# Windowed attention with global tokens, then a softplus MLP: indices spread by a product, q and k in one tile, V of batch 1 rounded by its transfer, and a new recorded order

## The chip, the cores and the metric

The kernel runs on one core of one Trainium2 chip. The core has five engines with an instruction stream each: PE (TensorE, matrix products), DVE (VectorE), ACT (ScalarE), POOL (GpSimd) and SP (SyncE, here used to issue transfers). The metric is the device time of one execution in microseconds; a comparison uses medians. Times inside an execution are read from a hardware profile of one execution, counted from the start of its span.

## The reference

Attention over 8 batches × 8 heads × 576 tokens × 64 dims: a token sees the 32 tokens to each side of it and 8 global tokens (the indices are an input), and the global tokens see all. Its output, 4608 tokens of 512 values, goes through a two-layer MLP with softplus.

```python
scores = scale * np.matmul(q, k.transpose(0, 1, 3, 2))
mask = np.abs(pos[:, None] - pos[None, :]) <= window       # window = 32
mask = mask | is_global[:, None] | is_global[None, :]
attn = np.exp(scores - max) / (sum + 1e-09)                # where the mask holds
x = (attn @ v).transpose(0, 2, 1, 3).reshape(B * S, H * D) # 4608 x 512
h = x @ w_in                                               # 512 x 2048
g = np.maximum(h, 0.0) + np.log1p(np.exp(-np.abs(h)))      # softplus
out = g @ w_out                                            # 2048 x 512
```

## The kernel before

**Tiles.** The tokens are cut into 36 "pairs" n of four blocks of 32 tokens (all 8 heads of a pair together) and nine MLP tiles m of 512 tokens, four pairs each. A batch has 18 blocks, so that batch 1 begins in the second tile.

**One pair.** PE makes the scores s (L1061, with a mask product at L1045 or L1055 for the first pairs). DVE adds the mask (L1065), takes the maximum m (L1076 or L1078), and after ACT's exponential (L1097 or L1101) the sum sm (L1108) and its reciprocal rs (L1110). POOL subtracts the maximum (L1084) and multiplies with the reciprocal (pn, L1116). DVE transposes the weights (pt, L1125), and PE multiplies them with V (xo, L1227): vb holds V of the window, vg the result of the global tokens.

**The global tokens.** Their q and k rows are picked by products with 0/1 matrices. Batches 0 and 1 are transposed on PE (tr, L843 and L846) and picked there with `hot` (L849, L853). From batch 2 on, DVE transposes q and k; PE picks the rows with `pick` (`pck`, L872: 18 products for k and 18 for q), a copy takes them to `picked`, and 32 small products with `place` (`put`, L886) lay them out; they are copied to `qg` (`gev`) and into the keys (`fill`). The global scores are sg (L959), their product with V is ov (L985).

**One MLP tile.** The four xo are copied to xT (L719). PE makes h in 16 chunks of 4 products (L1262), ACT the softplus g (L1268), PE the second product o in 4 × 16 products (L1273), and the copies osb go out by transfers (L1285). `PIECED` names the tiles whose h are made in pieces, as their pairs come in: tile 0 in pieces of 1, 2 and 1 pairs, tile 1 of 1 and 3, the others whole.

**Transfers.** SP issues the loads of q, k and v. Batches 0 and 1 come in parts (`load_part`, L511 for 256 tokens, L515 for the last 64), later batches in 32-token blocks (`load_qk`, L456; `load_v`, L466). POOL issues transfers through its software queue: V of batch 0, which is rounded to bf16 on the way (`load_rounded`, L461), the first weights win (L1325, four pieces) and the second weights wout (L1329, four pieces). V of batch 1 and later is loaded as it is into `stage` and cast on an engine (L719). Two tiny transfers called `trail` (L750, `follow`) read a piece of the weights, so that SP waits there: the first for the third piece of win ahead of the parts of batch 1, the second for the second piece of wout ahead of V of batch 1. A copy called `seen` (L1406, the job "landed") makes POOL wait for a part of batch 1 ahead of wout: the last 64 tokens of q, third among batch 1's loads in SP's order.

**The order.** All work is recorded as jobs, with engines that may run it, costs and due times, in class `_Order`. A table `ORDER` (one number for each job and the engine chosen) then fixes the order of everything. Where PE has nothing to do in the first microseconds, `fill_in` puts products without use (warm, L727), whose operand is the tile `pgt`.

## Time and profile before

| what | us |
|---|---|
| median of 3 runs (lowest, highest) | 333.86 (333.33, 334.97) |
| the profiled execution, its own time | 334.75 |
| its span in the profile | 333.0 |
| PE busy / DVE busy / ACT busy / POOL busy | 318.6 / 223.4 / 228.4 / 193.6 |
| first h of the MLP | 29.49 |
| scores of batch 1's first whole pair | 46.22 |
| PE idle before ov of batch 1 | 1.46 |
| moved by DMA, whole span | 42.14 MB |

The span runs from the first to the last instruction; 1.75 us of the profiled execution lie outside it. Rows of a timeline read: start, duration, engine, line, operation, output<-input, count, and in brackets how long the engine was idle before and what ended that. Durations of PE rows overlap, since its products are pipelined: what a product costs is read from start to start. Rows of a table of windows read: the stretch, its length, then busy time and count on PE, on PE's weight loads, on DVE, ACT and POOL, the granted clock, the DMA share and GB/s. The granted clock was 0.984 of full speed over the span, and full from 24 us on in every window that is shown.

### The profile page before, as it was taken

The numbers are of one execution on the slowest core, as the hardware profiler recorded it, in microseconds if no ns is written. First come the engines' busy times: TensorE is split into PE (matmuls) and PEld (weight loads), VectorE is DVE, ScalarE is ACT, GpSimd is POOL, SyncE is SP. The second block draws the span as 40 slices with busy tenths as digits, with TensorE's granted clock in tenths as the row PEclk, the third lists the DMA queues.
The fourth block names the chain that finished last, engine by engine and source line by source line (L and its number), as shares of the span: only waits on it lengthen the run. The fifth ranks groups of instructions, "written<-read, shape, count | busy, mean of one in ns | idle before, by whom it ended". The sixth has DMA issues, their size and how long they took to land.

```text
span 333.0 us, 12043 instructions
## 1 busy us (share of the span) xinstructions
PE 318.6 (96%) x5273; PEld 170.8 (51%) x5273; DVE 223.4 (67%) x393; ACT 228.4 (69%) x448; POOL 193.6 (58%) x171
## 2 busy tenths in 40 slices
PE   6978899899999999999999999999999999999995
PEld 2736785465555455544454445445544454454453
DVE  7689679895897899992884299497966757530000
ACT  3889866796787879388746664997369666743622
POOL 5976308694677778879639459587447445600000
PEclk9589999999999999999999999999999999999999
DMA  6999899999889999999950799520210002000102
GB/s 179 165 160 214 198 183 175 152 143 230 141 135 175 214 184 142 225 204 156 213 114 33 125 181 219 114 65 33 98 64 33 33 2 96 2 33 31 65 24 103
DMA packets 168796, 42.14 MB, mean 127 GB/s; under 512 B 153256, under 2 KB 165800, under 8 KB 168744
## 3 DMA queue, kind: packets, MB, share of 16 engines
q1 hardware_dynamic: 154888, 26.63, 44.7%
q0 software_dynamic: 10944, 11.08, 16.4%
q10 hardware_dynamic: 2912, 3.67, 3.1%
q8 instruction: 41, 0.67, 0.8%
q14 instruction: 11, 0.09, 0.1%
HBM read 36.71 MB, written 9.44 MB: 139 GB/s over the span
## 4 chain that ended last, share of the span: by engine, by line
PE 75%; DMA 6%; DVE 5%; SPq 4%; POOL 4%; issue 2%; ACT 2%; POOLq 0%
PE h L1262 32%; PE o L1273 32%; PE xo L1227 3%; DMA stage<-in_q_dram 3%; PE s L1061 3%; SPq L456 3%; DMA win<-in_moe_w_in_dram 2%; PE tr L843 1%; SPq L466 1%; POOL pn L1116 1%; PE ov L985 1%; DVE sm L1108 1%; DVE st L1065 1%; DMA gi<-in_global_idx_dram 1%; DVE m L1078 1%
## 5 line engine op out<-in xcount | busy, mean ns | idle before, releaser
L1273 PE MATMUL o<-wout,g 128*128 128x512 bf16 (+1 forms) x592 | 140.5, 374 | 0.3 <-ACT g L1268 0.3
L1262 PE MATMUL h<-xT,win 128*128 128x512 bf16 (+3 forms) x768 | 139.6, 326 | 0.9 <-ACT xT L719 0.8
L1268 ACT ACTIVATE g<-h 128x512 bf16<-128x512 f32 (+3 forms) x192 | 83.2, 504 | 44.1 <-PE h L1262 41.6
L1262 PEld LDWEIGHTS <-win 128*128 128x128 bf16 x768 | 66.6, 98 | 60.6 <-issue 2.2
L1273 PEld LDWEIGHTS <-g 128*128 128x128 bf16 x592 | 55.5, 98 | 60.7 <-ACT g L1268 2.0
L1116 POOL TENSOR_TENSOR pn<-st,rs 128x1024 bf16<-128x1024 f32 (+1 forms) x37 | 66.2, 1799 | 31.5 <-DVE rs L1110 23.5
L1084 POOL TENSOR_TENSOR st<-st,m 128x1024 f32<-128x1024 f32 x32 | 60.3, 1895 | 31.6 <-DVE m L1078 31.5
L1065 DVE TENSOR_TENSOR st<-s,mask 128x512 f32<-128x512 f32 x64 | 41.1, 674 | 12.2 <-PE s L1061 12.1
L1108 DVE TENSOR_REDUCE sm<-st 128x8 f32<-128x1024 f32 x32 | 38.3, 1198 | 6.6 <-ACT st L1101 6.5
L1078 DVE TENSOR_REDUCE m<-st 128x8 f32<-128x1024 f32 x32 | 38.3, 1204 | 0.2
L1101 ACT ACTIVATE st<-st 128x1024 f32<-128x1024 f32 x32 | 33.3, 1059 | 1.6 <-POOL st L1084 1.5
L1125 DVE STREAM_TRANSPOSE pt<-pn 128x512 int32<-128x512 int32 x36 | 24.5, 691 | 9.1 <-POOL pn L1116 9.0
L719 ACT COPY osb<-o 128x512 f32<-128x512 f32 (+1 forms) x27 | 15.7, 580 | 17.8 <-PE o L1273 15.9
L719 ACT CAST xT<-xo 128x512 bf16<-128x512 f32 (+3 forms) x25 | 11.0, 512 | 19.1 <-PE xo L1227 19.1
L719 POOL CAST vb<-stage 128x1152 bf16<-128x1152 f32 x12 | 13.6, 1144 | 14.3 <-DMA stage<-in_v_dram 10.2
L1268 ACT ACT_TABLE_LOAD x14 | 18.0, 1283 | 0.2
L1285 POOL DMA_DIRECT2D out_dram<-osb x24 | 13.7, 572 | 4.6 <-DMA stage<-in_k_dram 3.5
L719 DVE CAST xT<-xo 128x512 bf16<-128x512 f32 (+3 forms) x23 | 11.3, 533 | 7.2 <-PE xo L1227 7.2
L1061 PEld LDWEIGHTS <-qx 64*32 64x32 bf16 x1152 | 10.3, 92 | 9.0 <-issue 6.0
L1061 PE MATMUL s<-kx,qx 64*32 64x128 bf16 x1152 | 14.7, 225 | 0.0
L716 POOL TENSOR_SCALAR qb<-stage 128x1152 bf16<-128x1152 f32 (+1 forms) x8 | 11.0, 1385 | 5.8 <-DMA stage<-in_q_dram 2.6
L1101 ACT ACT_TABLE_LOAD x11 | 14.1, 1283 | 0.2
(125 smaller groups left out, 296.8 us busy)
## 6 DMA issues: line engine op xcount, KB each, us to landing
stage<-in_v_dram SPq DMA_DIRECT2D x56, 144.0 KB, 3.8
stage<-in_k_dram SPq DMA_DIRECT2D x48, 144.0 KB, 4.2
stage<-in_q_dram SPq DMA_DIRECT2D x48, 144.0 KB, 3.6
out_dram<-osb POOLq DMA_DIRECT2D x24, 256.0 KB, 3.4
out_dram<-osb ACTq DMA_DIRECT2D x11, 256.0 KB, 2.0
stage<-in_q_dram SPq DMA_DIRECT2D x4, 512.0 KB, 5.5
win<-in_moe_w_in_dram POOLq DMA_DIRECT2D x8, 256.0 KB, 6.1
wout<-in_moe_w_out_dram POOLq DMA_DIRECT2D x4, 512.0 KB, 9.0
```

Source lines behind the costliest of these rows:

```text
L719: {"ACT": nc.scalar.copy, "DVE": V.tensor_copy, "POOL": nc.gpsimd.tensor_copy}[e](out, in_)
L1061: nc.tensor.matmul(out=PS["s", n, g][quad(a), x, :], lhsT=qx[b % 2][rows(g), a, j * BL:(j + 1) * BL], rhs=kx[b % 2][rows(g), a, e0 * BL:(e ...
L1065: V.tensor_tensor(out=PS["st", n][:, h, :, :], in0=PS["s", n, h][:, :, :], in1=mask[:, h, j0:j0 + PB, :, :].rearrange("p j s i -> p j (s i ...
L1078: V.reduce_max(out=m[:], in_=flat(PS["st", n], h0, h1), axis=AX)
L1084: on(e).tensor_tensor(out=t, in0=t, in1=over(PS["m", n, y][:], SL * BL), op=OP.subtract)
L1101: nc.scalar.activation(out=t, in_=t, func=AF.Exp)
L1108: V.reduce_sum(out=sm[:], in_=flat(PS["st", n], h0, h1), axis=AX)
L1116: on(e).tensor_tensor(out=PS["pn", n][:, :, :, h0:h1].rearrange("p x s h -> p h x s"), in0=PS["st", n][:, h0:h1], in1=PS["rs", n, y][:].re ...
L1125: V.transpose(out=bass.AP(base.tensor, base.offset, ap=[list(base.ap[0]), [2 * STEP, PB // 2], [STEP + BL // 2, 2], [1, SL * BL]]), in_=PS ...
L1262: nc.tensor.matmul(out=h[:, :], lhsT=w_in_t[c // 4][:, kd, c % 4 * P:(c % 4 + 1) * P], rhs=PS["xT", m][:, kd, lo:hi], start=(kd == 0), sto ...
L1268: nc.scalar.activation(out=PS["g", m, c][:, lo:hi], in_=PS[key][:, lo_of(c, hi - lo)], func=AF.Softplus)
L1273: nc.tensor.matmul(out=PS["o", m, ns, a][:, :], lhsT=PS["g", m, kf][:, ns * P:(ns + 1) * P], rhs=w_out_t[kf // 4][:, kf % 4, a:z], start=( ...
```

## The change

1. The global indices come by one DMA of one partition on ACT's queue (it was one of 128 partitions on SP's). DVE splits them into bytes (`make_bytes`), PE spreads them to all partitions by a product with ones (`make_spread`), and `make_hot` puts the bytes together again. The first part of q is now first on SP; k's first part was on ACT's queue.
2. q and k lie in one tile `qk`. From batch 2 on, 16 products pick rows of both (256 columns) and four do the last chunks (128 columns): 20 instead of 36. `put` is one product of 256 columns with a 128×128 `place` in the stead of 32. A copy (`back`) takes the result to `placed`, a DVE transpose (`gev`) to `qkg`, and `fill` reads that.
3. V of batch 1 is rounded by its transfer: eight DMAs of POOL behind the fourth wout, and no cast. K of batch 2 waits on SP, by the second trail, for the fourth wout.
4. The gate of wout (`landed`) reads the part 1 of k, second among batch 1's loads in the new order.
5. `PIECED` has tile 2 as pieces of 1 and 3 pairs.
6. Warm products read a tile of their own (`idle`).
7. Some subtractions and products pn of tiles 0 to 3 may lie on DVE. Constants of the recorder are changed, and the table `ORDER` is new.

```diff
-    PIECED = {0: (1, 2, 1), 1: (1, 3)}
+    PIECED = {0: (1, 2, 1), 1: (1, 3), 2: (1, 3)}
     ORDER = (
-        4, 88, 52, 131, 9, 57, 112, 14, 137, 92, 116, 107, 62, 142, 148, 102, 188, 190, 126, 121, 217, 201, 97, 19,
+        52, 62, 57, 4, 65, 141, 126, 9, 136, 107, 147, 131, 72, 98, 102, 196, 152, 227, 112, 158, 200, 206, 122, 14,
...
-    gi = const([P, 2 * NG], I32, "gi")
-    qb = const([P, HG * NC, BL, 2], BF16, "qb")
-    kb = const([P, HG * NC, BL, 2], BF16, "kb")
+    gi = const([1, 2 * NG], I32, "gi")
+    gb = const([1, 2 * NG], BF16, "gb")
+    ones = const([1, P], BF16, "ones")
+    qk = const([P, 2, HG * NC, BL, 2], BF16, "qk")
+    qb, kb = qk[:, 0], qk[:, 1]
...
+    idle = const([P, 512], BF16, "idle")
...
-    place = const([P, R, 2 * NG], BF16, "place")
+    place = const([P, P], BF16, "place")
...
-    load_part(0, 1, 0, nc.scalar)
-    nc.sync.dma_start(out=gi[:, :], in_=global_idx.rearrange("(one n) -> one n", one=1).bitcast(I32)
-                      .to_broadcast([P, 2 * NG]))
+    load_part(0, 0, 0)
+    nc.scalar.dma_start(out=gi[:, :], in_=global_idx.rearrange("(one n) -> one n", one=1).bitcast(I32))
...
+    def make_bytes():
+        V.tensor_copy(gb[:].rearrange("p (n x) -> p n x", x=2),
+                      gi[:].bitcast(mybir.dt.uint8).rearrange("p (n x) -> p n x", x=8)[:, :, 0:2])
+
+    def make_spread():
+        PS["gi"] = psum(("gi",), [P, 512], FP32)
+        nc.tensor.matmul(out=PS["gi"][:, 0:2 * NG], lhsT=ones[:, :], rhs=gb[:, :], start=True, stop=True)
...
+    def add_rounded(b, deps):
+        T["cast", b, 2] = []
+        for c in range(R):
+            T["cast", b, 2].append(o.add({"POOL": (1360, 0)}, lambda e, c=c: load_rounded(b, c), T["cast", b, 2][-1:] or deps,
+                                         rank=-1, moves=1400, hold=0 if b or c else 8700))
+        T["load", b, 2] = T["cast", b, 2][-1]
...
+            def emit(e):
+                if b == EARLY and "led" not in T:
+                    T["led"] = True
+                    follow(1, w_out_t[KF // 4 - 1])
+                load_qk(nc.sync, b, w, (0, 2, 1, 3))
...
+        def pck(e):
+            PS[key] = psum(key, [P, 512], FP32)
+            x = qk[:].rearrange("p w (a c) i d -> p w a c i d", a=HG)
+            for t in range(2 * NC):
+                c, z = divmod(t, 2)
+                whole = t < 2 * NC - 2
+                for w in range(1 if whole else 2):
+                    n = t % R if whole else t % R + 2 * w
+                    w0, w1 = (0, 2) if whole else (w, w + 1)
+                    nc.tensor.matmul(out=PS[key][quad(n), w0 * P:w1 * P], lhsT=pick[:, c, z, :],
+                                     rhs=x[:, w0:w1, :, c, :, z] if whole else x[:, w, :, c, :, z], start=(t < R), stop=not whole)
...
+        def put(e):
+            nc.tensor.matmul(out=PS[key][:, 2 * P:4 * P], lhsT=place[:, :], rhs=picked[:].rearrange("p w d -> p (w d)"), start=True, stop=True)
+
+        def back(e):
+            copy(e, placed[:], PS[key][:, 2 * P:4 * P])
...
+                V.transpose(out=qkg[i][:].rearrange("p w a g -> p (w a g)"), in_=placed[:])
...
-            T["landed"] = o.add(pool(100), lambda e: nc.gpsimd.tensor_copy(seen[:, 0, :], natural(0, FULL)[:, 0:1]), [T["part", 1, 0, FULL]], rank=0)
+            T["landed"] = o.add(pool(100), lambda e: nc.gpsimd.tensor_copy(seen[:, 0, :], flat(stage[1])[:, 4 * HD - 1:4 * HD]), [T["part", 1, 1, 1]], rank=0)
```

The new table moves instructions at three places that matter below. The first is ACT's order around the first copy to xT, at 29 us: st, sm<-s, m are exponentials of tile 0, g the first softplus. Before:

```order
L971 ACTIVATE pg<-sg,gnb 128x256
L1097 ACTIVATE st,sm<-s,m 128x128 x24
L719 CAST xT<-xo 128x128 x3
L1268 ACT_TABLE_LOAD
L1268 ACTIVATE g_834<-h 128x128
```

and now:

```order
L995 ACTIVATE pg<-sg,gnb 128x256
L1121 ACTIVATE st,sm<-s,m 128x128 x16
L1020 ACTIVATE vg_75<-ov,grs 128x128
L739 CAST xT<-xo 128x128 x2
L1121 ACTIVATE st,sm<-s,m 128x128 x4
L1292 ACT_TABLE_LOAD
L1292 ACTIVATE g_914<-h 128x128
```

All 32 exponentials stood ahead of the xT casts; now 28 do, and the last four stand behind them, with vg ahead of them.

The second is SP's order from the first trail on (stage_60 is q, stage_61 k, stage_62 v). Before:

```order
L750 DMA trail<-win_127 1x2x1
L511 DMA stage_60<-in_q_dram 128x8x128
L511 DMA stage_61<-in_k_dram 128x8x128
L515 DMA stage_60<-in_q_dram 64x4x64 x2
L511 DMA stage_61<-in_k_dram 128x8x128
L515 DMA stage_61<-in_k_dram 64x4x64 x2
L511 DMA stage_60<-in_q_dram 128x8x128
L750 DMA trail<-wout_130 1x2x1
L466 DMA stage_62<-in_v_dram 32x18x64 x8
L456 DMA stage_61<-in_k_dram 32x36x32 x8
```

and now:

```order
L769 DMA trail<-win_132 1x2x1
L518 DMA stage_61<-in_k_dram 128x8x128 x2
L518 DMA stage_60<-in_q_dram 128x8x128 x2
L522 DMA stage_60<-in_q_dram 64x4x64 x2
L522 DMA stage_61<-in_k_dram 64x4x64 x2
L769 DMA trail<-wout_137 1x2x1
L458 DMA stage_61<-in_k_dram 32x36x32 x8
```

The big parts now come first and the tails last, V of batch 1 is gone, and the second trail reads the fourth piece of wout. On POOL the eight V transfers stand behind the four wout, ahead of the first subtraction of batch 1 (L1084, then L1108). Before:

```order
L1406 COPY seen<-stage_60 128x1
L1329 DMA wout_129<-in_moe_w_out_dram 128x4x512
L1329 DMA wout_130<-in_moe_w_out_dram 128x4x512
L1329 DMA wout_131<-in_moe_w_out_dram 128x4x512
L1084 TENSOR_TENSOR st<-st,m 128x1024 x2
L1329 DMA wout_132<-in_moe_w_out_dram 128x4x512
L719 CAST vb_67<-stage_62 128x18x64
L1084 TENSOR_TENSOR st<-st,m 128x1024
L719 CAST vb_67<-stage_62 128x18x64
```

and now:

```order
L739 CAST qk<-stage_61 128x2x4x64
L1431 COPY seen<-stage_61 128x1
L1353 DMA wout_134<-in_moe_w_out_dram 128x4x512
L1353 DMA wout_135<-in_moe_w_out_dram 128x4x512
L1353 DMA wout_136<-in_moe_w_out_dram 128x4x512
L1353 DMA wout_137<-in_moe_w_out_dram 128x4x512
L463 DMA vb_68<-in_v_dram 32x18x64 x8
L1108 TENSOR_TENSOR st<-st,m 128x1024 x3
```

The fourth wout no longer stands behind two subtractions, both casts of V are gone, and a cast of k stands ahead of `seen`.

The third is PE at the placing product of batch 2 (each product stands with its weight load). Before, the first two of the 32 behind the products h:

```order
L1262 MATMUL h<-xT,win_127 128x384
L886 LDWEIGHTS picked
L886 MATMUL pick<-place,picked 32x8
L886 LDWEIGHTS picked
L886 MATMUL pick<-place,picked 32x8
```

and now, all of it:

```order
L1286 MATMUL h<-xT,win_131 128x384
L906 LDWEIGHTS place
L906 MATMUL pick<-picked,place 128x256
L1286 LDWEIGHTS win_131
L1286 MATMUL h<-xT,win_131 128x384
```

Where 32 products of 8 or 16 columns stood, there is one of 256, between products h of the same kind as before.

More of the change, by code (lines that the diff above doesn't have):

```diff
@@ L721 @@
     o = _Order(SLOTS, KINDS, 8)
-    idle = pgt[:].rearrange("p m i -> p (m i)")
     def fill_in(key, n):
@@ L1416 @@
     o.follow(ORDER)
-    for job in o.run(dict(PE=1200 if WARM else 3000, ACT=2600, DVE=2100, POOL=3400, DMA=2700)):
+    for job in o.run(dict(PE=1200 if WARM else 3000, ACT=2600, DVE=2100, POOL=3400, DMA=2000)):
         job["emit"](job["on"])
```

123 lines of the change are left out of this document (54 added, 69 removed), and 144 rows, old and new, of the table ORDER.

## The prediction

> **What bounds the kernel now.** I read the page first (busy time, then the chain that ended last).
>
> ```profile
> PE 318.6 (96%) x5273; PEld 170.8 (51%) x5273; DVE 223.4 (67%) x393; ACT 228.4 (69%) x448; POOL 193.6 (58%) x171
> PE 75%; DMA 6%; DVE 5%; SPq 4%; POOL 4%; issue 2%; ACT 2%; POOLq 0%
> ```
>
> PE is busy for 96% of the span and holds 75% of the chain. So time can be won in two ways only: fewer PE microseconds, or fewer stretches in which PE has nothing useful. Where those lie is seen by stage (PE busy is the second column) and in the list of what PE waited for.
>
> ```profile
> 28.00:40.00 12.00, 10.20 (x234) 8.78 (x226) 9.64 (x26) 10.20 (x40) 5.64 (x11) 1.00 0.95 231
> 40.00:46.00 6.00, 5.43 (x150) 5.12 (x151) 3.33 (x9) 4.50 (x13) 0.00 (x0) 1.00 1.05 159
> 54.00:62.00 8.00, 6.89 (x92) 3.92 (x91) 7.90 (x13) 7.70 (x15) 4.21 (x4) 1.00 0.97 157
> 104.00:320.00 216.00, 216.00 (x3393) 106.52 (x3377) 140.36 (x213) 147.51 (x230) 126.70 (x90) 1.00 0.51 107
> PE ov L985 <- DVE m L1078: 1.5, 1, 1.5
> PE o L1273 <- ACT g L1268: 0.3, 1, 0.3
> ```
>
> From 104 us on PE is never idle: only its own work counts there. The open time lies ahead: 1.8 us from 28 to 40, 0.57 from 40 to 46, 1.1 from 54 to 62, and the two later waits listed (1.5, 0.3), to which a third, of 0.54, comes at 76 us (row at tile 2, below). What bounds the early part is when the first h and the scores of batch 1 can start.
>
> ```profile
> 29.49 4.03 PE L1262 MATMUL h<-xT,win 128*128 128x128 bf16 x64 [0.79 <-ACT xT L719]
> 46.22 0.78 PE L1061 MATMUL s<-kx,qx 64*32 64x128 bf16 x64
> ```
>
> The first h starts at 29.49; the scores of batch 1 at 46.22. Between them PE has too little it may do, so **work that is put ahead of 46.22 is won, and a shift of 46.22 is lost or won whole**. The sum below is made at that point.
>
> **The change, part by part.**
>
> *The first 29 us.* The indices come in one packet and are spread by a product instead of a DMA to all partitions.
>
> ```profile
> 0.81 3.60 DMA gi<-in_global_idx_dram
> 9.04 0.61 PE L843 MATMUL tr<-ident,qb 128*128 128x128 bf16 x4 [2.77 <-POOL qb L716]
> ```
>
> The index transfer lasts until 4.41, and it stands first in the chain; the first transposes wait for q until 9.04. Now q's first part is ahead of everything on SP and the indices are on ACT's queue; against that stand a cast on DVE and a small product with its wait. Bounds: −1 (some of the 2.77) and +1 (the new steps, if the indices end last at the mask). I count it as nothing, since the first h hangs on ACT's exponentials, which come next.
>
> *The scores of batch 1.* They need its loads, the casts and the transposes.
>
> ```profile
> 28.77 0.42 ACT L1097 ACTIVATE st<-s,m 128x128 f32<-128x128 f32 x1
> 29.11 0.66 ACT L719 CAST xT<-xo 128x128 bf16<-128x128 f32 x3
> 21.23 0.45 DVE L975 STREAM_TRANSPOSE pgt<-pg 128x256 bf16<-128x256 bf16 x1 [1.36 <-PE warm L727]
> ```
>
> ACT casts xT at 29.11, right behind its last exponential (28.77, one every 0.34 us, 28.77 to 29.11). The new order puts the last four behind the xT casts: up to 4 × 0.34 = 1.4 us earlier. The warm matmuls get a tile of their own, so DVE no longer waits 1.36 us at 21.23. These two overlap, and batch 0's own loads and an added PE-to-DVE index step stand ahead of both; I take h at 28 to 28.5. SP's loads of batch 1 hang on the third piece of the first weights, whose place hardly changes; so of the gain I carry only **−0.7** to the scores. Bounds: −1.2 (all of the ACT gain but 0.2) and, where the loads are slowed, +4 and beyond (rivals).
>
> *Work put ahead of those scores.* Counted in PE's order, 84 products h of 128 columns, 44 of 256 and no o stood ahead of them; now 80, 56 and five o of 512. The price is
>
> ```profile
> 106.59 3.45 PE h L1262 x16
> ```
>
> 0.216 us for 512 columns, so 0.054 and 0.108 for the narrow ones: 12 × 0.108 + 5 × 0.216 − 4 × 0.054 = 2.2 us. There is room: PE's idle 1.8 + 0.57 without the 0.79 ahead of h is 1.6 us, an h that starts 1 to 1.5 us earlier makes it 2.6 to 3.1, and 2.2 with the 0.7 of the scores take 2.9. **−2.2**; bounds 0 (h not earlier, so the work itself pushes the scores) and −2.2.
>
> *V of batch 1 by POOL's transfers, and the gate of the second weights.*
>
> ```profile
> 54.27 12.21 SPq L456 DMA_DIRECT2D stage<-in_k_dram x8
> wout<-in_moe_w_out_dram POOLq DMA_DIRECT2D x4, 512.0 KB, 9.0
> vb<-in_v_dram POOLq DMA_DIRECT2D x7, 72.0 KB, 3.4
> 61.16 1.14 POOL L719 CAST vb<-stage 128x1152 bf16<-128x1152 f32 x1 [3.67 <-DMA stage<-in_v_dram]
> 62.35 0.80 PE L985 MATMUL ov<-vb,pgt 32*32 32x129 bf16 x72 [1.46 <-DVE m L1078]
> 10.27 5.69 POOL L461 DMA_DIRECT2D vb<-in_v_dram x8
> ```
>
> The 1.46 us are put down to DVE, but POOL's second cast of V ends at 61.16 + 1.14 = 62.30 and the product starts at 62.35: V was late. Now V comes rounded behind wout on POOL's own queue: eight issues of 5.69 / 8 = 0.71 us, hidden under POOL's idle time ahead of its first subtraction,
>
> ```profile
> 49.83 3.75 POOL L1084 TENSOR_TENSOR st<-st,m 128x1024 f32<-128x1024 f32 x2 [9.92 <-DVE m L1078]
> q0 software_dynamic: 1576, 1.57, 102.9%
> q0 software_dynamic: 4848, 0.71, 150.8%
> ```
>
> (uncovered they would cost up to 5.7 us of POOL). The four wout are 2.1 MB; from 40 to 50 us the software queue moved 1.57 MB (upper row), so 13.4 us; with batch 0's V it moved 0.71 MB from 12 to 19 (lower row), so the eight pieces, 0.59 MB, take 5.8. With wout from about 39.5 V is there near 59, ahead of 62. The wait of ov goes, and two casts (2.3 us) leave POOL, and K of batch 2 (54.27), now behind the last wout instead of V, starts about where it did, since wout ends near 53. The 0.5 and 0.3 us stalls go with the new order. Of 1.5 + 0.5 + 0.3 I book **−2.0**; bounds 0 and −2.3.
>
> The Trainium skill ("DMA: Bandwidth & Descriptors", section "Queues, rings and completion order") says that each DMA engine serves the queues with work in turn, packet by packet, so the loads on SP would go on beside wout at a packet's share. The trace so far speaks rather for starving, in the two rows from 56 to 59 us quoted under the rivals; what the rule makes of the time is the second rival.
>
> *Picks of batches 2 to 7.*
>
> ```profile
> 104.85 0.47 PE L872 MATMUL pick<-kb,pick 128*32 128x128 bf16 x18
> 105.55 1.04 PE L1273 MATMUL o<-wout,g 128*128 128x512 bf16 x4
> 109.97 0.37 PE L886 MATMUL pick<-place,picked 128*32 128x8 bf16 x32
> 110.27 0.39 PE L1273 MATMUL o<-wout,g 128*128 128x512 bf16 x1
> ```
>
> Picking takes 0.70 us for 36 (19 ns each: four run side by side), placing 0.30 for 32. The new 16 × 256 + 4 × 128 columns cost 0.49 us if they stream at the full rate (a quarter of 0.108 and 0.054 each) and 0.69 if width counts as the 19 ns do; the one placing matmul of 256 columns 0.11. Gain per batch 0.20 to 0.40, six batches 1.2 to 2.4: **−1.5**, since the 19 ns look like a price per instruction for the larger part. The new copy and DVE's transpose (an estimate: half of the transpose of pt whose row stands under the rivals) add some 1 us a batch to DVE and ACT, beside a PE that is full, with DVE at 67%; uncovered, a batch's global scores would come 1 us later.
>
> *Tile 2 in two pieces.*
>
> ```profile
> 65.13 0.23 PE L1227 MATMUL xo<-pt,vg 32*64 32x64 bf16 x8
> 65.75 1.47 PE L1273 MATMUL o<-wout,g 128*128 128x512 bf16 x6
> 76.08 0.38 PE L1227 MATMUL xo<-pt,vg 32*64 32x384 bf16 x8 [0.54 <-DVE pt L1125]
> 77.31 1.68 PE L1273 MATMUL o<-wout,g 128*128 128x512 bf16 x7
> 103.36 1.56 PE xo L1227 x143
> ```
>
> Tile 1 already goes so: its xo took 0.62 + 1.23 = 1.85 us against 1.56 whole: +0.3. Its 64 products h of 512 columns become 128 of 384 and 128; at 2 to 4 ns more for each pair, +0.2. **+0.5** (0.3 to 0.8).
>
> *Stalls of the re-made order.* Every engine's order is new (a few subtractions and products of tiles 0 to 3 may now lie on DVE too), and waits of this size cannot be read from an order: **+1.5**, as much as the largest stall of now; bounds 0 and 3.
>
> **Sum:** −0.7 − 2.2 − 2.0 − 1.5 + 0.5 + 1.5 = −4.4. The profiled execution took 334.75, with a span of 333.0; by the sum it becomes 330.35 and 328.6. The median shown, 333.86, lies 0.89 lower: **329.5**.
>
> **The rivals.**
>
> *Starved loads (slower).* The gate of wout moves from the third of batch 1's six loads to the second.
>
> ```profile
> 37.13 0.26 POOL L1406 COPY seen<-stage 128x1 f32<-128x1 f32 x1 [6.08 <-DMA stage<-in_q_dram]
> q1 hardware_dynamic: 1393, 0.60, 76.0%
> q0 software_dynamic: 419, 0.42, 90.8%
> q1 hardware_dynamic: 238, 0.05, 12.0%
> ```
>
> Now wout is let go at 37.13, issued at 37.59, and until 40.4 SP's queue still moved 0.60 MB (first queue row), so that the loads ended just as wout began. An earlier gate lets wout in near 39, with 0.15 to 0.5 MB of them open. From 56 to 59 us, with both queues loaded, SP got 0.05 MB beside 0.42 (last two rows), 17 GB/s: 0.25 MB take 15 us, until 54, and the scores come near 56, 10 us late: −4.4 + 0.7 − 1.5 (PE waits, so the others catch up) + 10 = +4.8, so **338.7**. It decides for slower as soon as the scores are more than 6.9 us late. Against it: only a rest may be open by then. Chance 0.13.
>
> *Turn by turn (the rule named above).* SP's packets from 37.6 to 40.4 were 0.60 MB / 1393 = 430 bytes, wout's 0.42 MB / 419 = 1000. With a turn each SP keeps three tenths of some 165 GB/s, 50: 0.25 MB take 5 us instead of the 1.2 at the 0.60 MB in 2.8 us of that row, 4 us more, of which 3 reach the scores: −4.4 + 0.7 − 1.5 + 3 = −2.2, **331.7**. Chance 0.14.
>
> *The gain is given back at tile 1 (no change).* From its scores to its xo, DVE was the bound (7.90 of 8 us busy from 54 to 62). If that chain stays as long, work put ahead leaves PE short at 76 us: without the −2.2, and with the waits of 0.54 and 0.3 still there, −4.4 + 2.2 + 0.8 = −1.4, **332.5**. Against it: two POOL casts are gone. Chance 0.12.
>
> *Late weights pt (slower).* Later tiles get their transposed weights with little to spare:
>
> ```profile
> 137.09 0.71 DVE L1125 STREAM_TRANSPOSE pt<-pn 128x512 int32<-128x512 int32 x1 [0.33 <-POOL pn L1116]
> 138.26 0.29 PE L1227 MATMUL xo<-pt,vg 32*64 32x192 bf16 x8
> ```
>
> 0.46 us here. PE work that shrinks comes earlier, POOL and DVE work doesn't; 1 us on each of seven tiles makes 329.5 + 7 = **336.5**. Against it: POOL is busy for 58% only. Chance 0.09.
>
> **How the numbers follow.** Forecast 0.52 (its own range 326.5 to 332.0), rivals 0.13, 0.14, 0.12, 0.09. A measurement of this kernel tells about 0.5%, 1.67 us: faster is below 332.2, slower above 335.5. Faster: the forecast and most of turn by turn, 0.52 + 0.13 = 0.65. Same: the third rival, 0.12, and the mild ends of the others, 0.03. Slower: starving and late weights, 0.13 + 0.09, less their mild ends, 0.20. The range leaves out the worst of starving and gains beyond the bounds: 326.0 to 336.5.
>
> **What would show it.** Right: first h before 28.6, the scores of batch 1 at 45 to 46, no wait of its ov, picks of batches 2 to 7 at 0.5 to 0.7 us, PE full from 80 us. Wrong: wout packets while SP's loads of batch 1 stand still, transposes of batch 1 waiting for casts of late parts; or xo of tiles 2 to 8 waiting for pt; or a wait of DVE or POOL in tile 1 that gives the lead back by 78 us.

## The result, and the profile after

| | kernel before | changed kernel |
|---|---|---|
| median (lowest to highest), us | 334.06 (333.33 to 334.97), 4 runs | 330.71 (329.47 to 331.85), 4 runs |
| profiled execution, its span, us | 334.75, 333.0 | 331.00, 329.3 |
| first h | 29.49 | 24.89 |
| scores of batch 1 | 46.22 | 45.41 |
| ov of batch 1 | 62.35, after 1.46 idle | 59.81, no wait |

The ratio is 0.9898, with a 95% interval from 0.9853 to 0.9942: faster by 1.0%. Medians, ranges and ratios here leave out executions that took over 1.5% longer than the fastest of the same kernel. The forecast was 329.5, its range 326.0 to 336.5.

The page of the changed kernel, busy time and the chain that ended last:

```profile
PE 311.0 (94%) x5007; PEld 171.1 (52%) x5052; DVE 228.1 (69%) x402; ACT 228.1 (69%) x468; POOL 198.6 (60%) x180
PE 74%; ACT 9%; DMA 8%; issue 2%; DVE 2%; POOL 2%; SPq 1%; ACTq 0%
```

Two readings need care. PE shows 5007 products but 5052 weight loads, and each product has its load: 45 records of products are missing, so PE's 311.0 us is too low, and small holes in its row are not all idle time. And DMA's part of the chain has grown from 6% to 8%, ACT's from 2% to 9%.

PE's waits in the changed kernel (total, times, longest), the largest ones and the one of h:

```profile
PE o L1297 <- issue: 2.9, 18, 0.2
PE xo L1251 <- ACT vg L1020: 2.3, 2, 1.9
PE xo L1251 <- issue: 1.7, 3, 0.7
PE tr L867 <- DVE qk L739: 1.5, 2, 0.8
PE o L1297 <- DMA wout<-in_moe_w_out_dram: 0.7, 1, 0.7
PE h L1286 <- DVE xT L739: 0.3, 1, 0.3
```

The 18 equal holes of 0.16 on o are missing records. The waits of ov for V and of o for g are gone from the list. "xo <- issue" is new: three holes of up to 0.7 us, 1.7 in all, in which PE waits for nothing that the profile shows.

The four stages, as windows (columns as before):

```profile
28.00:40.00 12.00, 11.36 (x278) 10.20 (x277) 7.86 (x25) 9.44 (x36) 6.60 (x10) 0.96 0.99 233
40.00:46.00 6.00, 4.84 (x139) 3.65 (x137) 2.90 (x9) 3.34 (x10) 1.01 (x3) 1.00 1.23 200
54.00:62.00 8.00, 7.79 (x145) 4.26 (x145) 7.18 (x11) 7.92 (x17) 7.54 (x5) 1.00 0.93 162
104.00:320.00 216.00, 211.66 (x3128) 106.48 (x3155) 142.46 (x217) 144.10 (x232) 126.13 (x88) 1.00 0.48 101
```

From 28 to 40 PE is busy 1.2 us more than before, from 54 to 62 0.9 more. (The clock of 0.96 in the first row: it was at half until 29.1 us, so that some of the 1.2 is slower products. More on the clock stands behind the experiments with V.) But from 40 to 46, just ahead of the scores of batch 1, it is busy 0.6 less: a new hole. Its cause is in the timelines of the changed kernel, PE's first h and scores, and DVE's cast of the last part of batch 1's k (a "tail" of 64 tokens) between them:

```profile
24.89 2.35 PE L1286 MATMUL h<-xT,win 128*128 128x128 bf16 x24
43.74 0.29 DVE L739 CAST qk<-stage 128x256 bf16<-128x256 f32 x1 [2.60 <-DMA stage<-in_k_dram]
45.41 0.78 PE L1085 MATMUL s<-kx,qx 64*32 64x128 bf16 x64
```

The first h is 4.6 us earlier than before, the scores only 0.81: DVE stood 2.60 us for the last tail. The DMA queues show why. Packets, MB and share of the changed kernel from 38 to 42 us:

```profile
q0 software_dynamic: 610, 0.61, 94.5%
q1 hardware_dynamic: 520, 0.13, 24.2%
```

and of the kernel before from 34 to 38 us, where SP's queue loads batch 1 with no wout beside it:

```profile
q1 hardware_dynamic: 1981, 0.79, 76.3%
```

Alone the loads move 1981 packets in 4 us; beside wout they move 520, about one for each of wout's 610. That is the round by packets that the Trainium skill describes ("DMA: Bandwidth & Descriptors", section "Queues, rings and completion order"), the second rival of the prediction; this trace agrees. The loads are not starved, as the first rival had it, but the tails' packets are small (0.13 MB / 520 = 250 bytes against 1000), so turn for turn they get a sixth of the bytes.

### The profile page after: what moved, and what is told of

It is laid out like the page before. It is cut to its first block, busy times and chain, and to the rows that moved or that the text cites. A ratio compares the mean times of both kernels' runs of the same rounds, so it can differ in the third digit from the quotient of the medians.

```text
span 329.3 us, 11571 instructions
## 1 busy us (share of the span) xinstructions
PE 311.0 (94%) x5007; PEld 171.1 (52%) x5052; DVE 228.1 (69%) x402; ACT 228.1 (69%) x468; POOL 198.6 (60%) x180
## 4 chain that ended last, share of the span: by engine, by line
PE 74%; ACT 9%; DMA 8%; issue 2%; DVE 2%; POOL 2%; SPq 1%; ACTq 0%
PE h L1286 33%; PE o L1297 32%; DMA wout<-in_moe_w_out_dram 4%; ACT st L1121 3%; PE xo L1251 3%; PE s L1085 3%; DMA stage<-in_k_dram 2%; DMA stage<-in_q_dram 2%; PE ov L1009 1%; ACT st L1125 1%; ACT g L1292 1%; PE pick L899 1%; ACT L1292 1%; ACT L1125 1%; POOL wout L1353 1%
## 5 line engine op out<-in xcount | busy, mean ns | idle before, releaser
L1286 PE MATMUL h<-xT,win 128*128 128x512 bf16 (+3 forms) x826 | 141.4, 316 | 1.2 <-DVE xT L739 0.3
L1297 PE MATMUL o<-wout,g 128*128 128x512 bf16 (+1 forms) x556 | 134.2, 373 | 4.1 <-issue 2.9
L1292 ACT ACTIVATE g<-h 128x512 bf16<-128x512 f32 (+3 forms) x208 | 86.3, 479 | 40.7 <-PE h L1286 36.6
L1286 PEld LDWEIGHTS <-win 128*128 128x128 bf16 x832 | 72.8, 99 | 59.4 <-issue 1.8
L1108 POOL TENSOR_TENSOR st<-st,m 128x1024 f32<-128x1024 f32 x31 | 58.2, 1893 | 38.6 <-DVE m L1102 38.5
L1140 POOL TENSOR_TENSOR pn<-st,rs 128x1024 bf16<-128x1024 f32 (+1 forms) x35 | 62.2, 1790 | 17.3 <-ACT g L1292 7.5
L739 POOL CAST qk<-stage 128x1152 bf16<-128x1152 f32 (+1 forms) x10 | 13.9, 1406 | 5.7 <-DMA stage<-in_k_dram 5.7
L463 POOL DMA_DIRECT2D vb<-in_v_dram x16 | 11.1, 710 | 8.8 <-DMA wout<-in_moe_w_out_dram 8.8
L1251 PE MATMUL xo<-pt,vb 32*64 32x96 bf16 (+2 forms) x1328 | 14.4, 210 | 1.7 <-issue 1.7
L1251 PEld LDWEIGHTS <-vb 32*64 32x64 bf16 x1328 | 13.7, 103 | 2.6 <-issue 2.1
```

The lines of the kernel that those rows point to most:

```text
L739: {"ACT": nc.scalar.copy, "DVE": V.tensor_copy, "POOL": nc.gpsimd.tensor_copy}[e](out, in_)
L1108: on(e).tensor_tensor(out=t, in0=t, in1=over(PS["m", n, y][:], SL * BL), op=OP.subtract)
L1140: on(e).tensor_tensor(out=PS["pn", n][:, :, :, h0:h1].rearrange("p x s h -> p h x s"), in0=PS["st", n][:, h0:h1], in1=PS["rs", n, y][:].re ...
L1251: nc.tensor.matmul(out=PS["xo", v_, c][h * D:(h + 1) * D, (x - X0) * BL:(z - X0) * BL], lhsT=lhs, rhs=rhs, start=start, stop=stop)
L1286: nc.tensor.matmul(out=h[:, :], lhsT=w_in_t[c // 4][:, kd, c % 4 * P:(c % 4 + 1) * P], rhs=PS["xT", m][:, kd, lo:hi], start=(kd == 0), sto ...
L1292: nc.scalar.activation(out=PS["g", m, c][:, lo:hi], in_=PS[key][:, lo_of(c, hi - lo)], func=AF.Softplus)
```

## The experiments

All compute the whole reference. Where a range of runs is given, the kernel was timed in rounds against the kernel before; the others are one execution each.

**The gate of wout, later and earlier.** The rest of the changed kernel is untouched. In one version `seen` waits for the first part of q, one load later; in the other for the first part of k, one load earlier:

```diff
-flat(stage[1])[:, 4 * HD - 1:4 * HD]
+flat(stage[0])[:, 2 * HD - 1:2 * HD]    # later (e1, e11)
+flat(stage[1])[:, 2 * HD - 1:2 * HD]    # earlier (e2)
```

> The changed kernel with one edit: the copy that lets the second weights (wout) start waits for part 0 of q, the third load of batch 1 in SP's order, instead of part 1 of k, the second. Theory A (packets in turn): from the first packet of wout on, SP's loads move one packet for each of wout's, about 130 per us instead of some 460, so what counts is how many of batch 1's packets are left at that point. wout starts some 1.5 us later, fewer are left, and the cast of the last 64 tokens of k starts near 41 us instead of 43.74; the scores of batch 1 come 0.5 to 1.3 us earlier than 45.41, and the span falls by about 1 us. Theory B (starved): the loads get next to nothing while wout runs; then the later gate helps more, the cast comes near 39 us. Theory C (PE is full ahead of the scores anyway, and o needs wout): the cast may come earlier, but the scores stay at 45.4 or come up to 1 us later, as the o that stand ahead of them wait for wout; the span is the same or up to 1 us longer.

> The changed kernel with one edit: the copy that lets wout start waits for part 0 of k, the first load of batch 1. wout starts about 1 us earlier than in the changed kernel. Theory A (packets in turn): some 460 more packets of batch 1 are left and go at about 130 per us: the cast of the last tokens of k starts 2 to 3 us later than 43.74, the scores of batch 1 as much later than 45.41, the span 1.5 to 3 us longer. Theory B (starved): the loads wait until wout and V of batch 1 are through, near 51 us; scores past 52, span 6 us longer or more. Theory C (the loads don't decide): scores at 45.4 or earlier, since the o ahead of them get wout earlier; span the same or shorter.

> The changed kernel with the gate of wout at part 0 of q, once more and timed. Its first run took 0.69 us off the scores of batch 1 and 1.2 us off the span, in spite of 2.7 us in which PE waited in tile 0's xo for nothing that the profile shows. Theory A (fewer packets left when wout starts): median 0.3 to 1.5 us below the changed kernel's 330.71, ratio to before 0.984 to 0.990. Theory B (the gain was one execution's luck): ratio 0.990 to 0.994. If the wait in xo belongs to PE's supply of instructions (its end stood 1.2 to 1.5 us behind a 16 KB transfer of the instruction queue in every run so far), it is there again, of changing length, with that same distance.

Later: 329.76, span 328.1, scores 44.72. The version timed in five rounds has a median of 329.69 (328.82 to 331.07, 6 runs), ratio 0.9892 (0.9862 to 0.9922), scores 44.96. Earlier: 331.56, span 329.9, scores 47.47. DVE's timeline of the later gate (the timed version), then of the earlier one:

```profile
41.78 0.45 DVE L739 CAST qk<-stage 128x256 bf16<-128x256 f32 x1
```

```profile
42.76 0.29 DVE L734 TENSOR_SCALAR qk<-stage 128x256 bf16<-128x256 f32 x1 [1.39 <-DMA stage<-in_q_dram]
45.64 0.45 DVE L739 CAST qk<-stage 128x256 bf16<-128x256 f32 x1 [2.59 <-DMA stage<-in_k_dram]
```

One load later and the tail no longer waits (41.78); one earlier and it comes at 45.64 instead of 43.74. The place of the gate sets the end of batch 1's loads: −0.5 to −0.7 us and +2.06 at the scores. The span pays 0.6 of the 2.06; the rest was not followed up. That the later gate's time differs from the changed kernel's is not shown: the two intervals overlap almost wholly. Nor are the 0.5 to 0.7 us the gate's alone: in both profiles with the later gate the clock was full from the start until 329 us, in the changed kernel at half from 25.6 to 29.1, and they have a new hole of PE of 2.5 and 2.7 us (last section).

**What stands in front of q's first part.** In the kernel before, the first part of k goes to SP behind q's, and the index broadcast to ACT's queue:

```diff
-    load_part(0, 1, 0, nc.scalar)
-    nc.sync.dma_start(out=gi[:, :], in_=global_idx...to_broadcast([P, 2 * NG]))
+    load_part(0, 0, 0)
+    load_part(0, 1, 0)
+    nc.scalar.dma_start(out=gi[:, :], in_=global_idx...to_broadcast([P, 2 * NG]))
```

> The kernel before with one edit: the first part of k is issued on SP behind the first part of q, and the index transfer (still to 128 partitions) goes to ACT's queue, where the first part of k was. In the changed kernel POOL's first cast of q starts at 5.50 instead of 8.37 and the first h at 24.89 instead of 29.49. Theory A (two queues shared the engines): the first part of q landed late because the first part of k moved beside it; then here the cast starts near 5.5 to 6, V and the first weights are issued 2 to 2.7 us earlier, and the first h comes at 26.5 to 28. Theory B (the index broadcast in 128 packets held q up): the broadcast is still there, so the cast stays near 8 and h near 29.5. The span falls by at most 1.5 us under A, since the scores of batch 1 wait for loads as well.

q's first cast starts at 7.07 instead of 8.37, but the first h at 30.44 instead of 29.49, the scores at 48.42, and the time is 334.46 (span 332.8). The cast came between the two expectations, h later than both. PE's first transposes did start 1.3 us earlier (7.76 instead of 9.04), but PE then waited three times for the next parts of k and q (0.97, 0.66, 0.46), and its clock was at half from 9.9 to 20.2 us. So with q first and the broadcast kept, nothing is won in this one execution.

**The changed kernel with the index broadcast.** 128 partitions on ACT's queue, no spreading product:

```diff
-    gi = const([1, 2 * NG], I32, "gi")
+    gi = const([P, 2 * NG], I32, "gi")
...
-    nc.scalar.dma_start(out=gi[:, :], in_=global_idx...bitcast(I32))
+    nc.scalar.dma_start(out=gi[:, :], in_=global_idx...bitcast(I32).to_broadcast([P, 2 * NG]))
...
-        nc.tensor.matmul(out=PS["gi"][:, 0:2 * NG], lhsT=ones[:, :], rhs=gb[:, :], start=True, stop=True)
```

> The changed kernel with one edit: the indices are again sent to all 128 partitions by the DMA (on ACT's queue), and the byte cast, the spreading product and the two instructions that put the bytes together are left out (one cast instead). Theory A (the place of q's first part in the queues brought the early start): POOL's first cast of q stays at 5.5 (within 0.6) and the first h within 0.5 us of 24.89. Theory B (the single packet brought it): the cast goes back to 7.5 to 8.4 and h to 27 to 29.

> The changed kernel without the single packet (indices sent to 128 partitions by the DMA, no spreading product), once more and timed; its first run took 335.86 us. Theory A (the packet is worth in the changed kernel what it is worth before, 2 to 3 us, and V of batch 1 and the picks bring the rest): median 332 to 333.5, ratio to before 0.994 to 0.999. Theory B (without the packet the new order, with its early gate of wout, loses what V and the picks bring): median 334 to 336, ratio 1.000 to 1.007; then the single packet carries the whole gain and the other parts together nothing, as the early gate puts the last loads of batch 1 beside wout.

One execution took 335.86; five rounds gave 333.47 (331.81 to 335.81, 12 runs) beside 333.46 for the kernel before, ratio 1.0011 (0.9977 to 1.0044). First h 27.49, scores 49.01. Without the single packet, all the rest of the change together wins nothing that can be measured. q's first cast on ACT starts at 6.64 instead of 4.98, PE's first transposes at 7.33 instead of 5.66, and h 2.60 later. The DMA traffic from 1 to 5 us says how q came late; the changed kernel as it is, then with the broadcast:

```profile
DMA packets 1535, 0.78 MB, mean 194 GB/s; under 512 B 18, under 2 KB 1535, under 8 KB 1535
```

```profile
DMA packets 907, 0.40 MB, mean 101 GB/s; under 512 B 133, under 2 KB 907, under 8 KB 907
q1 hardware_dynamic: 778, 0.40, 40.0%
q10 hardware_dynamic: 129, 0.01, 1.8%
```

The broadcast is 129 packets of 64 bytes and 0.01 MB, 1.8% of the engines' time by the records; yet beside it the loads move half as much (0.40 MB instead of 0.78). What holds them is not in the records.

**The single packet alone, in the kernel before.** The edit is the change's own (one-partition `gi`, bytes, product with ones, put together in `make_hot`); of the warm products the first five stay and the others follow `make_hot`.

> The kernel before with one edit: the indices come in one packet on SP and are spread by a product of PE (between five and nine of the first warm products), as in the changed kernel; order, loads, picks and pieces as before. Theory A (the broadcast of 64 bytes to 128 partitions held up every load beside it, as from 1 to 5 us 0.78 MB moved with the single packet and 0.38 to 0.47 MB with the broadcast): the first cast of q starts 1.5 to 2.5 us earlier than 8.37, the first h and the scores of batch 1 come 1.5 to 3 us earlier than 29.49 and 46.22, and the median is 1.5 to 3 us below before: this part alone brings half or more of the 3.35 us of the whole change. Theory B (the loads after it bound the scores anyway, by the trail and the gate): h earlier, but the scores by less than 0.7 us, the median within 0.7 us of before.

331.31 (330.58 to 333.59, 9 runs), ratio 0.994 (0.9902 to 0.9977): 2.0 us. From 1 to 5 us 0.77 MB move, against 0.47 before; q is cast at 6.99, the first h starts at 27.41, the scores at 43.70, earlier than in the changed kernel. Its ov of batch 1 in PE's timeline:

```profile
60.67 0.80 PE L994 MATMUL ov<-vb,pgt 32*32 32x129 bf16 x72 [2.30 <-POOL vb L728]
```

Now that the scores come earlier, the wait for V is longer and is put down to POOL's cast of V, where the profile of before named DVE.

**V of batch 1 alone, in the kernel before.** Its loads no longer stand behind wout:

```diff
-                    if behind and h == 0:
-                        follow(1, w_out_t[1])
```

> The kernel before with one edit: SP does not wait for the second wout ahead of V of batch 1, so these eight loads are issued near 37 us instead of 48.6. Theory A (the 1.46 us that PE waited ahead of ov were V, not DVE's maximum): the last cast of V moves ahead of 60 us, and PE's wait ahead of ov of batch 1 falls below 0.3 us. Theory B (DVE's maximum ended last): the wait stays at 1.2 to 1.6 us. In both, V's loads share the engines with wout packet by packet, so o may wait for wout up to 2 us near 46, and the span is between 1.5 us shorter and 1.5 us longer.

331.39, span 329.7. Casts of V at 53.07 and 56.21 in place of one that began at 61.16; ov at 59.58 with no wait. So the 1.46 us were V's. The time of this one execution is not V's alone: its scores of batch 1 came at 44.97 instead of 46.22, and the edit changes nothing ahead of 35.9 us, where V's loads now begin.

**The clock in these runs.** What differs there is the granted clock. Windows from 9 to 19 us of the kernel before, of the one with V let free, and of the one with the single packet:

```profile
9.00:19.00 10.00, 9.96 (x191) 6.73 (x198) 7.72 (x22) 8.35 (x26) 9.86 (x16) 0.52 1.38 143
9.00:19.00 10.00, 9.04 (x212) 6.22 (x213) 8.24 (x23) 8.94 (x30) 9.92 (x16) 0.83 1.42 145
9.00:19.00 10.00, 8.27 (x211) 4.89 (x207) 9.09 (x27) 9.47 (x35) 10.00 (x16) 1.00 1.41 132
```

In the profile of before, PE ran at half its clock from 8.4 to 18.6 us, where it makes batch 0's transposes and scores: a group of four transposes and four picks took 0.54 us there, 0.33 in the kernel with the packet. With V let free the same code ran at half for 3.4 us in that stretch, and its first transposes (8.95 against 9.04), first h (28.60 against 29.49) and scores (44.97 against 46.22) drew ahead step by step. Against this execution, the single packet takes 1.27 us off the scores, not 2.5; its first transposes start only 0.40 earlier than before (8.64), and 2.24 more are won by the time the first warm products behind batch 0's scores start (16.59 instead of 19.23).

The timed runs agree. The mean clock over the span was 0.988 in 42 executions of the kernel before, 0.985 in 12 of the changed kernel with the broadcast, 0.995 with the single packet in the kernel before (9 executions) and 0.997 in the changed kernel (4). Among the 42 alone, 0.01 more clock goes with 1.8 us less time (over all kernels with several executions together, with 1.4). That makes it an estimate that about 1 of the packet's 2.0 us, and 1.3 to 1.7 of the whole change's 3.35, came with the clock. The packet goes with a fuller clock in two orders of work, so this is no mere luck of single runs; but how it does so is not shown. In the kernel before, its edit also moved nine warm products, which now fill PE's 2.77 us of waiting ahead of the transposes, and no run moved only those. Nor does a wait of PE alone decide: ahead of ov of batch 0 (near 21 us) PE waited 2.2 us with the packet, with V let free and with both; the clock fell behind it in the first two and not in the third.

**Both, and a warm tile of its own, in the kernel before.**

> The kernel before with two edits together: the indices in one packet, spread by a product, and V of batch 1 not held behind the second wout. Order, loads, picks and pieces as before. Alone, the first took 2.5 us off the scores of batch 1 (43.70) but left PE waiting 2.30 us for V ahead of ov; the second took that wait away. Theory A (these two are what the change is worth, the rest of it gives and takes): the wait ahead of ov falls below 0.3 us, the scores come at 43.5 to 44.5, and the median is 4 to 5.5 us below before: as fast as the changed kernel (ratio 0.9898) or faster. Theory B (V's loads beside wout slow the last loads of batch 1 and wout itself by packets in turn): scores at 45 or later or o waiting for wout, and the median at most 2.5 us below before.

> The kernel of the run before this one with a third edit: the warm products read a tile of their own, so that DVE doesn't wait for PE ahead of the transposes of the global weights (1.36 us in the kernel before). Theory A (that wait stands on the way to the first h): h starts 0.5 to 1.4 us earlier than with the two edits. Theory B (h hangs on ACT's 32 exponentials and the xT cast behind them): h within 0.4 us. The median moves by less than 1 us either way, since the scores of batch 1 hang on their loads too.

The two edits: 330.44 (329.59 to 332.23, 7 runs), ratio 0.9911 (0.9875 to 0.9946), less than the 4 to 5.5 us expected; scores at 44.16, no wait of ov. With the warm tile: 330.36 (329.41 to 332.17, 7 runs), 0.9903 (0.9867 to 0.9939). Two edits of the kernel before, with its old order, its 36 picks and tile 2 whole, give a time that can't be told from that of the whole change. The warm tile moves h from 27.20 to 25.93 and the time by nothing that can be told; of these 1.27 us, 0.58 are there already at the global scores of batch 0 (14.74 instead of 15.32), ahead of the wait that the edit removes, so that about 0.7 is the tile's; PE now waits for the first weights instead, here in the version with all three:

```profile
PE h L1270 <- DMA win<-in_moe_w_in_dram: 1.4, 2, 1.0
```

**The 36 picks back, in the changed kernel**, and the placing product as four of 32 columns' weights:

```diff
-                for w in range(1 if whole else 2):
-                    n = t % R if whole else t % R + 2 * w
+            for w in (1, 0):
+                for t in range(2 * NC):
...
-            nc.tensor.matmul(out=PS[key][:, 2 * P:4 * P], lhsT=place[:, :], rhs=..., start=True, stop=True)
+            for r in range(R):
+                nc.tensor.matmul(out=PS[key][quad(r), 2 * P:4 * P], lhsT=place[:, quad(r)], rhs=..., start=True, stop=True)
```

> The changed kernel with two edits: 36 picking products of 128 columns for batches 2 to 7 instead of 20, and the placing product cut into four that write 32 partitions each. In the changed kernel a batch's 20 picks took 0.64 us and the placing product 0.11 us, with about 0.2 us ahead of it; in the kernel before 0.70 and 0.30, with 0.5 from the last h to the first product. Theory A (what counts is the change of the array's shape, some 0.3 us each time PE goes from 128 x 128 products to ones of 32 columns): 36 picks take 0.70 here as before, and the four placing products 0.1 to 0.15 us, but with 0.4 to 0.5 us from the last h to the first of them; a batch takes 0.3 to 0.5 us more than in the changed kernel, the span 2 to 3 us more. Theory B (the number of products counts): picks 0.70, placing 0.2, no change of the gap ahead; a batch 0.15 us more, the span 1 us.

344.38, span 342.7: 13.4 us more, where the picks themselves cost 0.27 a batch more, 1.6 in all: between starts of weight loads picking takes 0.69, placing 0.23 and the change of array shape ahead of it 0.09, against 0.63, 0.11 and none. PE's waits and two rows of its timeline show where most of the rest lies:

```profile
PE o L1295 <- issue: 3.8, 2, 2.2
PE s L1083 <- issue: 2.8, 1, 2.8
PE xo L1249 <- issue: 2.1, 2, 1.7
```

```profile
109.84 0.60 PE L1295 MATMUL o<-wout,g 128*128 128x512 bf16 x2 [2.24 <-issue]
144.67 0.42 PE L1083 MATMUL s<-kx,qx 64*32 64x128 bf16 x20 [2.85 <-issue]
```

Five such holes, 8.8 us in all by the profile, in which PE waits for nothing that it shows (last section). The clock also fell to half for 3.4 us each near 46, 111 and 145 us, the last two right behind a hole. So this run prices the picks only by their rows, not by its time. It was not timed in rounds.

**The last four exponentials ahead of the xT casts again**, in the changed kernel (a job moved in the recorded order):

> The changed kernel with one edit: the last four exponentials of tile 0 stand ahead of the casts to xT again, as in the kernel before. Theory A (ACT's order sets the first h): h starts 1.0 to 1.4 us later than 24.89, since the xT cast had come at 24.63 after 0.77 us of ACT's idle time. Theory B (the product xo, late by vg, sets it): h within 0.3 us of 24.89. The scores of batch 1 hang on the last casts of its loads (43.74 in the changed kernel): under both they move by less than 0.7 us, and the span by less than 1 us, because what h starts later fills PE's idle time ahead of them.

332.38, span 330.7, first h as a stream 26.98 instead of 24.89, scores 47.67. PE's timeline:

```profile
26.98 2.29 PE L1286 MATMUL h<-xT,win 128*128 128x128 bf16 x20 [1.10 <-ACT xT L739]
```

h waits for ACT's xT again: the place of four activations is worth 1.1 us directly. Of the 2.1 at h, 0.35 are there already at tile 0's first xo (24.26 instead of 23.91), and the clock was at half from 25.0 to 31.8 us. Both expectations had the scores within 0.7 us; they came 2.26 later. DVE's cast of the last tail waited for its load until 45.90 (43.74 in the changed kernel), with wout let go as early as there (34.0) and SP's last tail issued 1.3 us later: the loads of batch 1 did not keep their place.

## Why the prediction was right, step by step

The forecast missed by 1.2 us and its sign and size held. Two of its steps failed, though, in opposite directions, and hid each other: the first 29 us gave more than was booked, and the loads of batch 1 took it back. (The new stalls took twice what was booked.) That the total came so near is in part luck.

**The first 29 us: failed.** The step was "I count it as nothing, since the first h hangs on ACT's exponentials, which come next", with bounds of ±1. The single packet alone is worth 2.0 us (ratio 0.994), and the changed kernel without it is no faster than the kernel before. Three things were missed. The broadcast was priced by its own length (0.81 to 4.41) and not by what it does to the loads beside it: 0.47 MB instead of 0.77 from 1 to 5 us. Work that starts earlier moves everything behind it, the exponentials too: with the packet alone h comes 2.08 earlier. And the clock had no term: PE of the kernel before ran from 8.4 to 18.6 us at half in its profile, with the packet it did not in that stretch. By the estimate above, that is about half of the 2.0 us; the loads alone are not shown to be worth them.

**The scores of batch 1, −0.7: size right, reasons half right.** −0.81 was measured. The two named causes are real: the exponentials (up to 1.7 at h, shown by putting them back) and the warm tile (about 0.7 at h, shown by adding it to the kernel before). But h came 4.6 earlier, not 1 to 1.5, and what was to hold the loads did not: "SP's loads of batch 1 hang on the third piece of the first weights, whose place hardly changes". SP's trail, which waits for that piece, ran at 24.94 instead of 27.30. With the packet alone the scores come at 43.70, 2.5 earlier. The changed kernel keeps 0.8, in part because its earlier gate lets wout into the loads; the later gate gives back 0.5 to 0.7 of the 1.7 us between, and the rest was not traced. The sum had no term for that; it stood among the rivals only, at 3 us for the scores. The two runs that move the gate price one load's place at 0.5 to 0.7 us (later) and 2.06 us (earlier). So the second rival's mechanism is at work inside the forecast's result.

**Work ahead of the scores, −2.2: right by the count.** The products that now stand ahead are worth 2.16 by their count and the forecast's price (no run takes them away again), and the room for them was there, more than was booked.

**V and the stalls, −2.0: right.** All three are gone, 2.3 us by the profile's idle. That V and not DVE ended the 1.46 is shown twice, by V's loads let free and by the wait of 2.30 put down to V's cast. V's last packets came near 54, not 59: the sum let wout begin at 39.5, and its first packets came near 36, as `seen` ran at 34.03. POOL's part went another way than argued, see the last section.

**Picks, −1.5: net right, its inside wrong.** Between starts of weight loads picking went from 0.69 (batches 2 and 3; 0.78 in two later ones) only to 0.63, so the time goes by columns and not by the "price per instruction" chosen; placing went from 0.30 to 0.11; and 0.1 us was won that was not in the sum, because the placing product now has the full array like the o and h around it, and no longer quarters of it. Together 0.35 a batch, 2.1 us. The new copy ahead of it costs back 0.4 between starts, once, as this row of the changed kernel's PE timeline shows, where one product o separates it from the picks:

```profile
103.36 0.27 PE L906 MATMUL pick<-picked,place 128*128 128x256 bf16 x1 [0.23 <-ACT picked L739]
```

**Tile 2, +0.5: about right.** Its xo, in two pieces, take 0.53 + 1.22 us instead of 1.56: +0.2. Its h in pieces were not measured apart.

**New stalls, +1.5: too low.** Counted between starts of weight loads (the profile's idle is shorter, since the modelled end of a product runs into it) they are 3.0 us, the upper bound: 0.6 for vg at 63.08, 0.4 at the placing product of 103.36, 0.5 for xT at 106.56, and 0.6 and 0.9 at two holes in PE's instructions, here in its timeline:

```profile
199.87 0.40 PE L1251 MATMUL xo<-pt,vb 32*64 32x96 bf16 x33 [0.42 <-issue]
235.33 0.25 PE L1251 MATMUL xo<-pt,vb 32*64 32x64 bf16 x15 [0.69 <-issue]
```

**The sum.** Span: −0.81 at the scores, −2.16 of work ahead and −0.7 behind, −3.7 in all against −4.4. The −0.81 is between two single executions, with the clock at half for 10.2 us ahead of the scores in one and 3.4 in the other. Behind the scores −1.5 was forecast. Counted in the same way, the rows give −2.7 (the three stalls gone) − 2.1 + 0.2 + 3.0 = −1.6; of that 0.9 did not arrive and is not accounted for.

**The other rivals.** Starved loads fell (520 packets moved beside wout). The gain was not given back at tile 1: PE is busy 7.79 of 8 us there. Late weights pt are not among PE's waits. What stays open: whether the new order or tile 2 in pieces wins anything by itself, since each would need an order table of its own, and it wasn't tried.

## What to carry to other kernels

Price a small transfer by what the loads and the work behind it lose, not by its own bytes or its length: the packet of indices alone gave 2.0 of the 3.35 us here, without it nothing was left of them, and it looked like nothing. Read the granted clock stage by stage in both profiles before a gain is put down to transfers: here about half of the packet's gain went with it. When a gate lets a large stream of big packets start, count the small packets that are still open behind it: they get one packet for each of the stream's, so the gate belongs behind the last load that is wanted soon. And if an edit moves the start of everything, follow each later wait from its new time before any is called unchanged.

## What the runs showed of the hardware that was not expected

**PE can run out of instructions.** Every hole put down to "issue" that is longer than 0.25 us, in all of these runs, ends 1.2 to 1.6 us behind the end of one transfer of the instruction queue. In the run with 36 picks such transfers ran from 107.49 to 108.42 and from 141.83 to 143.42, and PE went on at 109.84 and 144.67. By the profile's idle they sum to 0 in the kernel before, 1.8 us in the changed one, 3.4 in the timed run with the later gate, 8.8 with the 36 picks. With the later gate the largest lies soon after the first h, in that run's PE timeline:

```profile
30.81 0.48 PE L1251 MATMUL xo<-pt,vb 32*64 32x96 bf16 x37 [2.48 <-issue]
```

The Trainium skill ("Runtime: NRT & Kernel Launch", section "Instruction fetch mechanics") says that each engine's instructions are refilled in blocks of 16 KiB and that the cost of crossing a block is mostly hidden. The size agrees (the queue's 39 transfers moved 0.64 MB in the changed kernel); the hiding does not hold at these holes. Most lie in or just behind a row of many short products, but the kernel before has such rows too, and no hole. The tie to the transfers is by their times alone and was not tested by itself.

**The clock falls to half for whole steps of 3.41 us.** In the clock records of all these runs, every stretch at half ahead of 320 us lasts 3.41, 6.83 or 10.24 us. The kernel before spent 10.24 that way, the changed kernel 3.41, the one with 36 picks four times 3.41. It cost time where PE was what the others waited for: 0.54 instead of 0.33 us for a group of transposes and picks.

**With eight software transfers open, the ninth waits.** POOL's timeline of the changed kernel behind the gate:

```profile
34.27 3.21 POOL L1353 DMA_DIRECT2D wout<-in_moe_w_out_dram  x4
37.46 2.69 POOL L463 DMA_DIRECT2D vb<-in_v_dram  x4
43.02 0.66 POOL L463 DMA_DIRECT2D vb<-in_v_dram  x1 [2.87 <-DMA wout<-in_moe_w_out_dram]
50.92 0.66 POOL L463 DMA_DIRECT2D vb<-in_v_dram  x1 [1.92 <-DMA wout<-in_moe_w_out_dram]
51.59 5.61 POOL L1108 TENSOR_TENSOR st<-st,m 128x1024 f32<-128x1024 f32 x3
```

Four wout and four pieces of V are issued in one go; each of the other four pieces waits for one wout to end. Whether the queue itself or the semaphores that the built program gives to it set this limit of eight is not shown. While it waits there POOL does nothing else, and its first subtraction of batch 1 started 2.65 us behind the maximum that it needs (48.94). No wait of PE came of it, because V and the scores were early enough.
